# Result tiles of an expert mixture: two stores of 64 queries each in place of one store over both row numbers

## The chip, the cores and the metric

The kernel runs on one core of a Trainium2 chip. The metric is the time of one execution on the device in microseconds, the median of several runs. The engines are named as the profile names them: PE (TensorE, matrix multiplication; PEld is its weight load), DVE (VectorE), ACT (ScalarE), POOL (GpSimd) and SP (SyncE, which here only issues DMAs). A core has 16 DMA engines, which carry out what SP issues.

## The reference

Three stages follow each other. Linear attention over 4 batches, 8 heads, 576 positions and 64 channels; then a gated two-layer block on the 2304 tokens; then a mixture of four experts, each weighted by the token's normalised domain probability.

```
attn:  kv = k_s^T v  per batch and head;   out = q_s kv
x = attn_out.transpose(0, 2, 1, 3).reshape(2304, 512)
moe:   h = (x @ w1) * (x @ w2) @ w3;   x = h @ w_out
moe2:  p = domain_probs / sum;   for each expert e of 4:
         out += p[:, e] * (relu(x @ e1[e]) @ e2[e])
```

The result has 2304 rows of 512 float32.

## The kernel before

**Passes.** The change lies in the last stage, the experts, from about 484 us on. The 2304 tokens are worked in three groups (`pr` = 0, 1, 2) of 768 tokens, and each group takes 8 passes (`NGE` = 8: four experts, the hidden width in two parts). So there are 24 passes `n`. A pass has `layer1(n)` (lines 727 to 786, matmuls at line 765) and `layer2(n)` (lines 788 to 814, matmuls at lines 112 to 114). `layer2` goes over the group's six result tiles in the order 3, 4, 5, 0, 1, 2; for each it adds the pass's part into the tile `acc[T]` (128 partitions of 512 float32, 256 KB) on DVE, at line 802 in a group's first pass and at line 806 in the others. In a group's last pass (n = 7, 15, 23) the tile is complete and `store(T)` is called at line 811.

**Weights.** `load_e(n)` (lines 555 to 565) brings a pass's weights by four DMAs of 512 KB on SP's queue: two of `e1r` (line 561), two of `e2r` (line 564). Both share three buffers (pool `raw`), so a load waits until an older one has been split. `e1_steps(n)` (line 694) splits `e1r` into high and low parts `eg`, on ACT at line 107 and on DVE at line 108; the matmuls of `layer1` read these. At a group's change `tset` (line 567) brings the next group's tokens, `yp` (line 571).

**Order.** A scheduler of the framework fixes each engine's order when the program is built, and an engine works through its own list in that order. SP does likewise: a DMA that is issued late holds up those behind it in SP's list, the weight loads among them. In the list the stores of a group stand together, ahead of the loads of `e1r` and `e2r` for the pass after next; the third group's stores end the program.

**Rows of the result.** A row number `n` of 0 to 8 and a query number `q` of 0 to 63 give one of a batch's 576 rows, row 9q + n. A tile holds two row numbers, 2t and 2t + 1, with 64 queries each: partitions 0 to 63 and 64 to 127. In DRAM the 64 rows of one row number lie 9 rows (18 KB) apart. `store(t)` therefore writes a view in which the row number is the first dimension: 2 x 64 x 512, from a tile of 128 x 512. Where the two row numbers belong to two batches (tiles 4 and 13 of 18), it writes two halves of 64 x 512 instead.

Of the kernel before, what the change touches and what calls it, by code (L numbers as in the profile page):

```python
# [61 lines left out]
def linear_attention_moe_kernel(ctx: ExitStack, tc, q, k, v, w1, w2, w3, wo, dp, e1, e2, out):  # L62
    nc = tc.nc
    w1, w2, w3, wo = (w.bitcast(I32) for w in (w1, w2, w3, wo))
    B, H, S, D = q.shape
# [9 lines left out]
    QP, QR = 64, 9  # L75
# [290 lines left out]
    def rows_cols(unit):  # L366
        c, kt = unit
        return ((kt,), 0) if c == "A" else ((kt, kt + 1), 4 if c == "B" else 6)
# [3 lines left out]
    for unit in UNITS:  # L372
        kts, _ = rows_cols(unit)
# [4 lines left out]
    n = 0  # L378
# [224 lines left out]
    for u, unit in enumerate(UNITS):  # L603
# [9 lines left out]
        for x, kt in enumerate(kts):  # L613
            for y in range(ni):
                i = i0 + y
# [65 lines left out]
    acc = {}  # L681

    def store(t):
        rows = [(2 * t + hf) for hf in range(2)]
        (b0, n0), (b1, _) = (divmod(i, QR) for i in rows)
        if b0 == b1:
            dst = out[S * b0:S * b0 + S].rearrange("(q n) d -> n q d", n=QR)
            nc.sync.dma_start(out=dst[n0:n0 + 2], in_=acc[t])
        else:
            for hf, i in enumerate(rows):  # L690
                dst = out[S * (i // QR):S * (i // QR) + S].rearrange("(q n) d -> n q d", n=QR)
                nc.sync.dma_start(out=dst[i % QR], in_=acc[t][QP * hf:QP * hf + QP])

    def e1_steps(n):

# [92 lines left out]
    def layer2(n, h, steps):  # L788
        w, pr, e = ew[n], n // NGE, n % NGE // 2
        order = [3, 4, 5, 0, 1, 2]  # L790
        for x, tt in enumerate(order):
            th, o = tt // 3, P * (tt % 3)
            T = 6 * pr + tt
            ps = bank(ps_h, "op")
            for i, (hf, u) in enumerate(((0, 0), (0, 1), (1, 0), (1, 1))):
                g, wg = h[u, hf, th], w["e2", hf, u]
                mm3(
                    ps, g[:, 0, o:o + P], g[:, 1, o:o + P], wg[:, 0], wg[:, 1], i == 0, i == 3
                )
            if n % NGE == 0:  # L800
                acc[T] = acp.tile([P, DM], F32, tag="acc", name="acc")
                nc.vector.tensor_scalar(
                    out=acc[T], in0=ps, scalar1=prob[:, T, e:e + 1], scalar2=None, op0=ALU.mult
                )
            else:
                nc.vector.scalar_tensor_tensor(  # L806
                    out=acc[T], in0=ps, scalar=prob[:, T, e:e + 1], in1=acc[T],
                    op0=ALU.mult, op1=ALU.add,
                )
            if n % NGE == NGE - 1:  # L810
                store(T)
            for f in steps[len(steps) * x // 6:len(steps) * (x + 1) // 6]:
                for g in f:
                    g()
# [44 lines left out]
```

## Time and profile before

| what | value |
|---|---|
| time, median of 3 runs | 1251.23 us (1251.16 to 1251.36) |
| the profiled execution | 1249.22 us |
| its span, first to last instruction | 1247.4 us |
| mean granted TensorE clock | 0.98 |
| PE busy | 1168.6 us, 94% of the span |
| DVE, ACT, POOL busy | 748.0, 497.6, 56.2 us |
| stores of results (256 KB; 128 KB) | 16; 4 |

The span is divided by stages: attention and the folding of the weights at first, the gated block to about 484 us, the experts after that. Times in the rows below are counted from the start of the span. "Idle before" an instruction is time in which its engine did nothing else, with the instruction or DMA that ended the wait behind the arrow. For SP the number behind a DMA's start is how long its issue held SP, not how long the transfer took. The DMA share of a window is the mean busy share of the 16 DMA engines.

### The profile page before, as it was taken

The page shows a single profiled execution, that of the slowest core. Times are in us where ns is not written, and L with a number is a line of the kernel's source. Part 1 is how long each engine was busy: PE and PEld are TensorE (multiplying, and loading weights), DVE is VectorE, ACT ScalarE, POOL GpSimd, SP SyncE. Part 2 cuts the span into 40 slices and gives each one's busy share as a digit, 9 for nine tenths or more (in the row PEclk, how much of TensorE's full clock was granted, in tenths as well). Part 3 has the DMA queues.
Part 4 walks back from the last instruction along what each step waited for, and adds up shares of the span by engine and source line. Part 5 has one row for each costly group of instructions (what it writes and reads, how often), then busy time and mean ns, then how long its engine had stood idle before and what let it go on. Part 6 is the DMA issues. An engine that isn't in the chain of part 4 may idle for free.

```text
span 1247.4 us, 15277 instructions
## 1 busy us (share of the span) xinstructions
PE 1168.6 (94%) x5728; PEld 1015.7 (81%) x5728; DVE 748.0 (60%) x1332; ACT 497.6 (40%) x1084; POOL 56.2 (5%) x76
## 2 busy tenths in 40 slices
PE   4789989999999999999999979999999799999994
PEld 3567868788878988999999979999999689999983
DVE  7988953423152147666667856666678376666641
ACT  4676544323241244333335433333344243333320
POOL 0020322201100000000000000000000000000000
PEclk9899999999999999999999989999999999999997
DMA  9949656527346431212121422211222312212001
GB/s 315 335 109 267 218 183 190 150 94 256 112 136 228 152 127 68 69 68 68 68 68 68 142 95 68 68 68 68 68 68 72 110 49 68 70 69 67 21 1 50
DMA packets 98394, 142.63 MB, mean 114 GB/s; under 512 B 26384, under 2 KB 63760, under 8 KB 98320
## 3 DMA queue, kind: packets, MB, share of 16 engines
q1 hardware_dynamic: 98320, 141.65, 34.6%
q8 instruction: 45, 0.74, 0.2%
q14 instruction: 29, 0.24, 0.1%
HBM read 123.81 MB, written 17.83 MB: 114 GB/s over the span
## 4 chain that ended last, share of the span: by engine, by line
PE 85%; DMA 7%; ACT 3%; DVE 2%; SPq 1%; issue 1%; POOL 0%; ACTq 0%; DVEq 0%; POOLq 0%
PE hp L765 26%; PE op L114 11%; PE op L112 11%; PE op L113 11%; PE ab L112 5%; PE ab L114 5%; PE ab L113 5%; PE y L112 2%; PE y L114 2%; PE y L113 2%; DMA e1r<-in_moe_w_dram 2%; PE kv L241 1%; DMA kr<-in_k_dram 1%; DMA f<-in_moe_w_dram 1%; ACT qe L270 1%; PE xp L318 1%
## 5 line engine op out<-in xcount | busy, mean ns | idle before, releaser
L765 PE MATMUL hp<-t,eg 128*128 128x384 f32 x2016 | 369.5, 335 | 3.3 <-DVE eg L108 2.1
L765 PEld LDWEIGHTS hp<-t,eg 128*128 128x128 f32 x2016 | 352.5, 188 | 14.7 <-DVE eg L108 2.7
L112 PE MATMUL op<-e2g,h 128*128 128x512 f32 x576 | 227.4, 395 | 15.0 <-ACT h L744 15.0
L113 PE MATMUL op<-e2g,h 128*128 128x512 f32 x576 | 227.7, 395 | 0.0
L114 PE MATMUL op<-e2g,h 128*128 128x512 f32 x576 | 223.8, 396 | 0.0
L740 ACT ACTIVATE p<-hp 128x384 f32<-128x384 f32 x144 | 65.2, 491 | 301.6 <-PE hp L765 301.6
L806 DVE SCALAR_TENSOR_TENSOR acc<-op,prob,acc 128x512 f32<-128x512 f32 x126 | 94.4, 749 | 128.8 <-PE op L114 125.2
L108 DVE TENSOR_TENSOR eg<-e1r,eg 128x512 fp32r<-128x512 f32 x168 | 114.7, 689 | 82.5 <-ACT eg L107 82.5
L107 ACT ACTIVATE eg<-e1r 128x512 fp32r<-128x512 f32 x168 | 104.9, 630 | 110.9 <-PE hp L765 47.5
L112 PEld LDWEIGHTS op<-e2g,h 128*128 128x128 f32 x576 | 109.3, 190 | 36.1 <-ACT h L744 15.7
L114 PEld LDWEIGHTS op<-e2g,h 128*128 128x128 f32 x576 | 109.2, 190 | 23.0
L113 PEld LDWEIGHTS op<-e2g,h 128*128 128x128 f32 x576 | 109.2, 190 | 21.0
L112 PE MATMUL ab<-x,wg 128*128 128x512 f32 (+1 forms) x320 | 120.9, 379 | 2.3 <-ACT ah L485 1.2
L113 PE MATMUL ab<-x,wg 128*128 128x512 f32 (+1 forms) x320 | 119.5, 373 | 0.0
L114 PE MATMUL ab<-x,wg 128*128 128x512 f32 (+1 forms) x320 | 119.1, 372 | 0.0
L753 DVE TENSOR_TENSOR p<-hp,p 128x384 f32<-128x384 f32 x144 | 79.6, 554 | 17.4 <-ACT p L740 17.2
L486 DVE TENSOR_TENSOR ah<-ab,ah 128x512 f32<-128x512 f32 (+1 forms) x40 | 25.3, 634 | 96.3 <-PE ab L114 87.2
L745 DVE SCALAR_TENSOR_TENSOR h<-p,h 128x384 fp32r<-128x384 f32 x144 | 76.3, 553 | 0.4
L744 ACT ACTIVATE h<-p 128x384 fp32r<-128x384 f32 x144 | 71.8, 514 | 7.8 <-DVE p L753 6.7
L112 PEld LDWEIGHTS ab<-x,wg 128*128 128x128 f32 x320 | 60.5, 189 | 14.8 <-ACT ah L485 2.4
L114 PEld LDWEIGHTS ab<-x,wg 128*128 128x128 f32 x320 | 60.6, 189 | 10.9 <-DVE wg L108 0.5
L113 PEld LDWEIGHTS ab<-x,wg 128*128 128x128 f32 x320 | 60.7, 190 | 10.0 <-DVE x L108 0.4
(86 smaller groups left out, 1273.6 us busy)
## 6 DMA issues: line engine op xcount, KB each, us to landing
wg<-w SPq DMA_DIRECT2D x64, 512.0 KB
e1r<-in_moe_w_dram SPq DMA_DIRECT2D x48, 512.0 KB
e2r<-in_moe_w_dram SPq DMA_DIRECT2D x48, 512.0 KB
f<-in_moe_w_dram SPq DMA_DIRECT2D x32, 512.0 KB
w<-wg SPq DMA_DIRECT2D x16, 512.0 KB
qr<-in_q_dram SPq DMA_DIRECT2D x16, 288.0 KB
yp<-yd SPq DMA_DIRECT2D x3, 1536.0 KB
f<-in_moe_w_out_dram SPq DMA_DIRECT2D x8, 512.0 KB
```

What stands on the lines that cost most here:

```text
L107: i = nc.scalar.activation(out=hi, in_=src, func=ACTF.Copy)
L108: eng.tensor_tensor(out=lo, in0=src, in1=hi.bitcast(F32), op=ALU.subtract)
L112: nc.tensor.matmul(out=ps, lhsT=w_hi, rhs=r_hi, start=first, stop=False)
L113: nc.tensor.matmul(out=ps, lhsT=w_hi, rhs=r_lo, start=False, stop=False)
L114: nc.tensor.matmul(out=ps, lhsT=w_lo, rhs=r_hi, start=False, stop=last)
L486: nc.vector.tensor_tensor(out=ah[:, 1, 0:n], in0=pss[1][:, 0:n], in1=ah[:, 0, 0:n], op=ALU.mult)
L740: nc.scalar.activation(out=p, in_=src, func=ACTF.Copy)
L744: nc.scalar.activation(out=g[:, 0], in_=src, func=ACTF.Relu)
L745: nc.vector.scalar_tensor_tensor(out=g[:, 1], in0=src, scalar=0.0, in1=g[:, 0].bitcast(F32), op0=ALU.max, op1=ALU.subtract,)
L753: nc.vector.tensor_tensor(out=p, in0=src, in1=p, op=ALU.add)
L765: nc.tensor.matmul(out=o, lhsT=wl[2 * sw + kt], rhs=t[b][:, kt, st], start=new and kt == 0 and i == 0, stop=kt == 1 and i == 2, skip_group ...
L806: nc.vector.scalar_tensor_tensor(out=acc[T], in0=ps, scalar=prob[:, T, e:e + 1], in1=acc[T], op0=ALU.mult, op1=ALU.add,)
```

## The change

`store` no longer asks whether both row numbers lie in one batch. It issues two DMAs for every tile, one for each row number, each from 64 partitions of the tile to 64 rows of the result.

```
     def store(t):
-        rows = [(2 * t + hf) for hf in range(2)]
-        (b0, n0), (b1, _) = (divmod(i, QR) for i in rows)
-        if b0 == b1:
-            dst = out[S * b0:S * b0 + S].rearrange("(q n) d -> n q d", n=QR)
-            nc.sync.dma_start(out=dst[n0:n0 + 2], in_=acc[t])
-        else:
-            for hf, i in enumerate(rows):
-                dst = out[S * (i // QR):S * (i // QR) + S].rearrange("(q n) d -> n q d", n=QR)
-                nc.sync.dma_start(out=dst[i % QR], in_=acc[t][QP * hf:QP * hf + QP])
+        for hf in range(2):
+            b, n = divmod(2 * t + hf, QR)
+            dst = out[S * b:S * b + S].rearrange("(q n) d -> n q d", n=QR)
+            nc.sync.dma_start(out=dst[n], in_=acc[t][QP * hf:QP * hf + QP])
```

The lists of PE, DVE, ACT and POOL are the same before and after. On SP, at the end of the first token group, these rows stood before (`out_dram<-acc` is a store, `yp<-yd` the next group's tokens):

```order
L561 DMA e1r<-in_moe_w_dram 128x4x256 x2
L571 DMA yp<-yd 128x4x768
L564 DMA e2r<-in_moe_w_dram 128x2x512 x2
L688 DMA out_dram<-acc 2x64x512
L692 DMA out_dram<-acc 64x512 x2
L688 DMA out_dram<-acc 2x64x512 x4
L561 DMA e1r<-in_moe_w_dram 128x4x256 x2
L564 DMA e2r<-in_moe_w_dram 128x2x512 x2
```

On SP at the same place now:

```order
L561 DMA e1r<-in_moe_w_dram 128x4x256 x2
L571 DMA yp<-yd 128x4x768
L564 DMA e2r<-in_moe_w_dram 128x2x512 x2
L687 DMA out_dram<-acc 64x512 x12
L561 DMA e1r<-in_moe_w_dram 128x4x256 x2
L564 DMA e2r<-in_moe_w_dram 128x2x512 x2
```

Seven stores have become twelve of one shape, at the same place in the list. At the end of the program SP's list read:

```order
L561 DMA e1r<-in_moe_w_dram 128x4x256 x2
L564 DMA e2r<-in_moe_w_dram 128x2x512 x2
L688 DMA out_dram<-acc 2x64x512 x4
L692 DMA out_dram<-acc 64x512 x2
L688 DMA out_dram<-acc 2x64x512
L854 UNCONDITIONAL_BRANCH
```

And on SP at the end of the program now:

```order
L564 DMA e2r<-in_moe_w_dram 128x2x512 x2
L561 DMA e1r<-in_moe_w_dram 128x4x256 x2
L564 DMA e2r<-in_moe_w_dram 128x2x512 x2
L687 DMA out_dram<-acc 64x512 x12
L849 UNCONDITIONAL_BRANCH
```

Here too twelve half stores stand where five whole ones and two halves stood. At the end of the second group, which has no tile across a batch, six whole stores have become twelve halves.

## Rows read from the trace of the kernel before

**Rows 1.** Page, part 1: busy time (share of the span) and instructions.

```profile
PE 1168.6 (94%) x5728; PEld 1015.7 (81%) x5728; DVE 748.0 (60%) x1332; ACT 497.6 (40%) x1084; POOL 56.2 (5%) x76
```

**Rows 2.** Waits of PE, 484 to 1248 us: total us, times, longest.

```profile
PE op L112 <- ACT h L744: 15.0, 2, 8.6
```

**Rows 3.** Timeline, PE: start, us, engine, line, operation, tiles, count [idle before].

```profile
737.05 0.79 PE L112 MATMUL op<-e2g,h 128*128 128x512 f32 x1 [6.34 <-ACT h L744]
...
997.74 0.80 PE L112 MATMUL op<-e2g,h 128*128 128x512 f32 x1 [8.63 <-ACT h L744]
```

**Rows 4.** Timeline, ACT: splits of e1r in both pauses and in another pass.

```profile
735.96 0.63 ACT L107 ACTIVATE eg<-e1r 128x512 fp32r<-128x512 f32 x1 [10.20 <-DMA e1r<-in_moe_w_dram]
...
996.65 0.63 ACT L107 ACTIVATE eg<-e1r 128x512 fp32r<-128x512 f32 x1 [13.18 <-DMA e1r<-in_moe_w_dram]
...
765.78 0.63 ACT L107 ACTIVATE eg<-e1r 128x512 fp32r<-128x512 f32 x1 [0.39 <-PE hp L765]
```

**Rows 5.** Timeline, SP: DMA issues, 691 to 1022 us.

```profile
691.01 0.92 SPq L561 DMA_DIRECT2D e1r<-in_moe_w_dram  x2
...
705.18 1.91 SPq L692 DMA_DIRECT2D out_dram<-acc  x2
711.04 10.80 SPq L688 DMA_DIRECT2D out_dram<-acc  x4
721.94 6.70 SPq L561 DMA_DIRECT2D e1r<-in_moe_w_dram  x2
...
761.76 0.92 SPq L561 DMA_DIRECT2D e1r<-in_moe_w_dram  x2
...
792.92 1.02 SPq L561 DMA_DIRECT2D e1r<-in_moe_w_dram  x2
...
949.35 0.92 SPq L561 DMA_DIRECT2D e1r<-in_moe_w_dram  x2
...
961.53 19.82 SPq L688 DMA_DIRECT2D out_dram<-acc  x6
981.44 8.01 SPq L561 DMA_DIRECT2D e1r<-in_moe_w_dram  x2
...
1021.90 0.92 SPq L561 DMA_DIRECT2D e1r<-in_moe_w_dram  x2
```

**Rows 6.** Windows: us, busy time of five engines, PEclk, DMA share, GB/s.

```profile
716.00:721.00 5.00, 5.00 (x24) 4.21 (x23) 2.80 (x5) 2.35 (x4) 0.00 (x0) 1.00 0.13 51
...
1233.00:1234.50 1.50, 0.00 (x0) 0.00 (x0) 0.00 (x0) 0.00 (x0) 0.00 (x0) 0.87 0.82 178
1234.50:1236.00 1.50, 0.00 (x0) 0.00 (x0) 0.00 (x0) 0.00 (x0) 0.00 (x0) 0.50 0.34 76
...
1246.00:1247.40 1.40, 0.00 (x0) 0.00 (x0) 0.00 (x0) 0.00 (x0) 0.00 (x0) 0.50 0.02 6
```

**Rows 7.** Windows over the two stretches at half clock (columns as above).

```profile
735.75:742.58 6.83, 5.53 (x13) 4.37 (x14) 4.68 (x9) 2.83 (x6) 0.00 (x0) 0.50 0.08 28
991.75:1001.99 10.24, 4.25 (x10) 3.42 (x11) 4.61 (x8) 2.84 (x6) 0.00 (x0) 0.50 0.39 136
```

**Rows 8.** Tail: SP and DVE in the timeline, and one window.

```profile
1217.47 9.88 SPq L688 DMA_DIRECT2D out_dram<-acc  x4
...
1233.09 0.55 SPq L688 DMA_DIRECT2D out_dram<-acc  x1
...
1226.44 0.75 DVE L806 SCALAR_TENSOR_TENSOR acc<-op,prob,acc 128x512 f32<-128x512 f32 x1 [1.97 <-PE op L114]
1229.16 0.75 DVE L806 SCALAR_TENSOR_TENSOR acc<-op,prob,acc 128x512 f32<-128x512 f32 x1 [1.97 <-PE op L114]
...
1218.00:1219.00 1.00, 1.00 (x7) 0.81 (x6) 0.72 (x1) 0.00 (x0) 0.00 (x0) 1.00 0.05 12
```

**Rows 9.** Instructions on tile acc: duration ns min/median/max, first and last start.

```profile
L688 SPq DMA_DIRECT2D out_dram<-acc x16: 512/540/2848, 703.2 to 1233.1; - x16
L692 SPq DMA_DIRECT2D out_dram<-acc x4: 542/954/4917, 705.2 to 1232.4; - x4
```

## Prediction

> **What bounds the kernel now.** I read the page first: TensorE is busy for 1168.6 us, 94% of the span [rows 1]. So TensorE is the bound nearly everywhere, and a change to stores can pay only where TensorE stands still. The stores come in the expert part, from 484 us on. There the table of waits has one line for TensorE: 15.0 us in two waits [rows 2]. The timeline gives their places: 6.34 us of idleness end at 737.05 and 8.63 us end at 997.74 [rows 3]. Both matmuls wait for ScalarE, and ScalarE in its turn had stood for 10.20 and 13.18 us on the DMA that brings e1r, the expert weights of the next pass [rows 4]. After 1229.9, when the last addition into acc ends, no engine works, and the span runs on for 17.5 us, to 1247.4 [rows 6, 8]. So there are three places: two pauses in the middle and the tail.
>
> All three lie behind stores. The timeline of SP's queue shows six result tiles stored at 703 to 722, six at 961 to 981, six at 1217 to 1234 [rows 5, 8, 9]. In the windows a whole-tile store keeps 0.13 of the DMA engines busy and moves 51 GB/s [rows 6]: 0.13 of 16 is two engines. A tile of 256 KB (262,144 bytes) then takes 262,144 / 51,000 = 5.14 us. A group holds five or six of these, 26 or 31 us on the same two engines, and the loads of e1r behind them need all engines. Their issue takes 6.70 and 8.01 us instead of 0.92, so the queue itself is held up [rows 5].
>
> **What a half tile does** is shown too, since tiles 4 and 13 of 18 cross a batch and are stored in two halves already (L692). When the two halves of tile 13 get their turn in the tail, the windows show 0.82 of the engines busy and 178 GB/s, then 0.34 and 76 GB/s, then the two-engine picture again [rows 6]. Half tiles therefore use all engines, and the pair takes about 3.0 us (1233 to 1236), beside a backlog on two engines.
>
> **The change, part by part.**
>
> *Order.* Compute on TensorE, VectorE, ScalarE and GpSimd keeps its order; only SP differs, with twelve half stores per group where six or seven transfers stood. Sixteen issues more.
>
> *Issues added.* A whole store's issue takes 540 ns at the median, a half's 954 ns over four, among them 4917 ns for one that stood behind four whole stores [rows 8, 9]; the least are 512 and 542 ns [rows 9]. The undisturbed pair cost 1.91 us [rows 5]. Taking 0.55 to 0.95 us for each, 16 more make 9 to 15 us on SP's queue. That lies beside work: in a group the six tiles come over 18 us as VectorE finishes them, and SP waits between. What stands behind the waiting SP are the e1r and e2r loads. Only the second half of the last tile delays them, 0.55 to 0.95 us: the first e1r load moves from 721.94 to about 722.7.
>
> *First pause.* Elsewhere a load of e1r issued at 761.76 is used at 765.78, 4.02 us later, and ScalarE's wait there is for TensorE and not for the DMA [rows 4, 5]. So the load issued at 722.7 is there at 726.7, or at 729.7 if it stands behind the whole 3.0 us of the last pair. ScalarE starts to wait at 735.96 - 10.20 = 725.76. Its 10.20 us cost TensorE 6.34, so 3.86 us of its waiting are free: TensorE notices nothing until 729.6. The pause goes entirely, at the worst all but 0.1 us.
>
> *Second pause.* The same with 13.18 - 8.63 = 4.55 us free. ScalarE starts to wait at 983.47; the load would be issued near 981 and arrive at 985 to 988, against a limit of 988.0.
>
> *What the pauses cost in all.* After them TensorE's granted clock is 0.50, that is 1.2 of 2.4 GHz, and TensorE works 5.53 and 4.25 us at it [rows 7]. The whole price shows in the distance between e1r loads. One pass takes 792.92 - 761.76 = 31.16 us. The two passes from 691.01 to 761.76 take 70.75, that is 8.43 over 62.32; the two from 949.35 to 1021.90 take 72.55, that is 10.23 over [rows 5]. Together **18.7 us**. Bounds: idleness plus half of the slow stretch, 14.97 + 0.5 x 9.78 = 19.9; idleness alone less 1 us for each load that comes late, 13.0. I take 18.7, since it is a distance measured over the whole disturbance. With no idleness I expect no drop of the clock either: both slow stretches begin in or just before the end of a pause [rows 3, 7].
>
> *Tail.* Now: the last whole store is issued at 1233.09, queued behind the others, and the last bytes go at about 1246.2 (6 GB/s over the last 1.4 us are 8.4 KB, 0.16 us at 51 GB/s) [rows 6, 8]. After the change the pair of the last tile is issued at 1229.94 and 1230.5, when the acc is ready; hardly anything is queued any more, since a pair is gone in 3.0 us and tiles come 1229.16 - 1226.44 = 2.72 us apart [rows 8]. First bytes come 1.3 us after an issue: 1217.47, and 12 KB moved by 1219, at 51 GB/s a quarter of a microsecond [rows 8]. Bounds for the bytes: 1.5 us for 256 KB at the 178 GB/s of the window, so the end at 1229.94 + 1.3 + 1.5 = 1232.7; or 3.0 us counted from the second half's first bytes, 1230.5 + 1.3 + 3.0 = 1234.8. I take 1234.2, near the slow end, because that row is the pair itself. What follows the last byte (1.2 us) stays. Gain 1246.2 - 1234.2 = **12.0 us**, bounds 11.4 and 13.5.
>
> *Sum.* 18.7 + 12.0 = 30.7 us off the profiled execution of 1249.22, which is its span of 1247.4 and 1.8 around it: 1218.5. The median is 1251.23, 2.0 above that execution, so **1220.5 us**. Own range: gains of 13.0 + 11.4 = 24.4 to 19.9 + 13.5 = 33.4 us, so 1217.8 to 1226.8.
>
> **A rule that speaks against it.** Rows 6 show one tile on two engines and its halves on nearly all. The Trainium skill (DMA: Bandwidth & Descriptors, Rules for kernel authors) says of two transfers to disjoint partition halves not to bother, because both spread over all 16 engines anyway and serialize, and to use one transfer over 128 partitions. By that rule the sum would be zero and the time that of rival B; its reason, a whole transfer on 16 engines, is not what this trace shows.
>
> **The rivals.**
>
> *A: the pauses stay, only the tail gains.* The table of waits could mislead, and e1r could be late for its buffer or for HBM traffic. For it: in every pass the load is issued only 4 us before its use. Against it: in both pauses the load had been issued 14.0 and 15.2 us before its use, and the two engines were full. Price: 12.0 us alone, 1239.2 us.
>
> *B: no gain, because a pair is no faster than a tile.* The mechanism: the rate is set by something that all stores share, the writing of 2 KB rows 18 KB apart in HBM, and not by the number of engines. Then halves go at 51 GB/s together, the bytes and the backlog stay, and one more issue of 0.6 us stands at the end: 1251.8 us. Against it: 178 GB/s in rows 6 with the same rows and the same stride.
>
> *C: slower, because a half store blocks SP.* If 4.92 us is what a 16-engine store's issue costs [rows 9], and not the backlog before it, twelve take 59 us from the first store at 703.2 [rows 9] and e1r is issued at 762 instead of 722. It arrives at 766, 30 us after 735.96, twice; the tail ends about 30 us later as well: some 1340 us. It decides from the mean issue: above (731.9 - 703.2) / 12 = 2.4 us the load comes later than now (731.9 is 735.96 less the 4.02). Against it: the pair at 705.18 took 1.91 us for both.
>
> *D: slower, because the rate goes with the size*, a half of 128 KB taking the 5.14 us of a whole. Twelve halves occupy the engines for 62 us per group instead of 26 to 31, and each of the three places is 31 to 36 us later: some 1350 us. Rows 6 speak against it as against B.
>
> **How the numbers follow.** Forecast 0.84, A 0.06, B 0.04, C 0.04, D 0.02. Faster by over 0.2% (2.5 us, about what a measurement can tell from no change): forecast and A, 0.90. Within: B, 0.04. Slower: C and D, 0.06. The range needs 0.8; the forecast's own bounds hold nearly all of its 0.84, so I give 1217.5 to 1227.0.
>
> **What would show it.** In the new profile: no wait of TensorE over 1 us after 484 us, and no stretch at 0.50 between 484 us and the end of compute; e1r loads 31 to 32 us apart throughout, also near 722 and 950; issues of e1r under 1.5 us; the DMA share in the store groups in short bursts over 0.5 and never 0.13 for microseconds on end; span end less than 6 us after the last addition into acc. If the pauses remain with an idle SP queue, A is right; if the share stays at 0.13, B; if issues of half stores take over 2.4 us each, C. The forecast is wrong in size if the load in the second pause comes after its limit of 988 by the new timeline's count, or if the last pair needs much more than 4.3 us from its first issue.

## The result, and the profile of the changed kernel

The changed kernel takes 1219.11 us (median of 4 runs, 1217.84 to 1220.65), the kernel before 1251.20 us (median of 4 too). The ratio is 0.9745 with a 95% interval of 0.9728 to 0.9762. The profiled execution took 1217.84 us, with a span of 1216.1 us.

The page of the changed kernel, parts 1 and 2 (busy time; then the clock granted to TensorE in 40 equal slices of the span, in tenths of full speed):

```profile
PE 1166.0 (96%) x5728; PEld 1014.4 (83%) x5728; DVE 750.4 (62%) x1332; ACT 497.7 (41%) x1084; POOL 52.4 (4%) x76
...
PEclk9889998999999999999999999999999999999999
```

Against [rows 1], TensorE's busy time is nearly the same; the span has lost what stood beside it. After 484 us the table of TensorE's waits, which had one line with 15.0 us in [rows 2], is empty. The windows of us, busy times of five engines, clock, DMA share and GB/s, first round the first change of token group, then round the second:

```profile
690.00:762.00 72.00, 72.00 (x367) 65.57 (x367) 55.13 (x94) 34.91 (x67) 0.00 (x0) 1.00 0.39 121
...
950.00:1022.00 72.00, 72.00 (x360) 64.64 (x359) 49.91 (x85) 27.61 (x56) 0.00 (x0) 1.00 0.31 95
```

The same windows of the kernel before:

```profile
690.00:762.00 72.00, 65.66 (x317) 58.57 (x316) 46.48 (x78) 27.51 (x54) 0.00 (x0) 0.95 0.30 103
...
950.00:1022.00 72.00, 63.37 (x307) 56.43 (x306) 42.07 (x72) 25.03 (x52) 0.00 (x0) 0.93 0.23 81
```

TensorE is now busy in all of the 72 us, at a granted clock of 1.00, which is 2.4 GHz; before it stood still for 6.3 and 8.6 us and the mean clock was 0.95 and 0.93. The queue of SP in the changed kernel (start, how long the issues held SP, line, tiles, count), which answers to [rows 5]:

```profile
661.62 0.92 SPq L561 DMA_DIRECT2D e1r<-in_moe_w_dram  x2
...
693.44 0.92 SPq L561 DMA_DIRECT2D e1r<-in_moe_w_dram  x2
...
705.62 19.25 SPq L687 DMA_DIRECT2D out_dram<-acc  x12
724.97 1.13 SPq L561 DMA_DIRECT2D e1r<-in_moe_w_dram  x2
...
755.02 0.92 SPq L561 DMA_DIRECT2D e1r<-in_moe_w_dram  x2
...
942.61 0.92 SPq L561 DMA_DIRECT2D e1r<-in_moe_w_dram  x2
...
954.79 18.21 SPq L687 DMA_DIRECT2D out_dram<-acc  x12
973.09 1.33 SPq L561 DMA_DIRECT2D e1r<-in_moe_w_dram  x2
...
1004.24 0.92 SPq L561 DMA_DIRECT2D e1r<-in_moe_w_dram  x2
```

Read the loads of e1r behind the stores: their two issues hold SP for 1.13 and 1.33 us, where it had been 6.70 and 8.01 us. The two passes from 693.44 to 755.02 take 61.58 us (70.75 before), those from 942.61 to 1004.24 take 61.63 us (72.55 before): 9.17 and 10.92 us, together 20.1 us.

The instructions on the tile acc (duration in ns, min/median/max; under them us from issue to landing), which answer to [rows 9], and the windows and the last addition of the tail, which answer to [rows 6, 8]:

```profile
L687 SPq DMA_DIRECT2D out_dram<-acc x36: 466/569/766, 705.6 to 1212.8; - x36
...
DMA to landing us min/median/max: 2.2/2.4/3.5
```

```profile
715.00:717.00 2.00, 2.00 (x14) 2.00 (x13) 0.00 (x0) 1.33 (x4) 0.00 (x0) 1.00 0.86 199
717.00:721.00 4.00, 4.00 (x20) 3.33 (x19) 1.44 (x2) 0.99 (x4) 0.00 (x0) 1.00 0.04 9
...
1213.00:1215.00 2.00, 0.00 (x0) 0.00 (x0) 0.00 (x0) 0.00 (x0) 0.00 (x0) 1.00 0.56 131
1215.00:1216.10 1.10, 0.00 (x0) 0.00 (x0) 0.00 (x0) 0.00 (x0) 0.00 (x0) 0.61 0.00 0
...
1211.51 0.75 DVE L801 SCALAR_TENSOR_TENSOR acc<-op,prob,acc 128x512 f32<-128x512 f32 x1 [1.97 <-PE op L114]
```

Stores are now short bursts (0.86 of the engines, 199 GB/s, then almost nothing) where 0.13 and 51 GB/s had gone on for tens of microseconds. The last addition ends at 1212.26 and the span at 1216.1: the tail is 3.8 us, before it was 17.5.

### The profile page after: what moved, and what is told of

It reads as the page before. It is cut to its first block, busy times and chain, and to the rows that moved or that the text cites. A ratio compares the mean times of both kernels' runs of the same rounds, so it can differ in the third digit from the quotient of the medians.

```text
span 1216.1 us, 15296 instructions
## 1 busy us (share of the span) xinstructions
PE 1166.0 (96%) x5728; PEld 1014.4 (83%) x5728; DVE 750.4 (62%) x1332; ACT 497.7 (41%) x1084; POOL 52.4 (4%) x76
## 4 chain that ended last, share of the span: by engine, by line
PE 88%; DMA 4%; ACT 4%; DVE 2%; SPq 1%; issue 1%; ACTq 0%; DVEq 0%
PE hp L760 28%; PE op L114 11%; PE op L113 11%; PE op L112 11%; PE ab L112 5%; PE ab L114 5%; PE ab L113 5%; PE y L112 3%; PE y L114 2%; PE y L113 2%; DMA kr<-in_k_dram 2%; PE kv L241 1%; DMA f<-in_moe_w_dram 1%; PE xp L318 1%; ACT qe L270 1%; DMA f<-in_moe_w_out_dram 1%
## 5 line engine op out<-in xcount | busy, mean ns | idle before, releaser
L114 PEld LDWEIGHTS op<-e2g,h 128*128 128x128 f32 x576 | 108.1, 188 | 22.5
L113 PEld LDWEIGHTS op<-e2g,h 128*128 128x128 f32 x576 | 108.1, 188 | 20.7
L112 PEld LDWEIGHTS op<-e2g,h 128*128 128x128 f32 x576 | 108.1, 188 | 20.0
```

The source lines that it names most:

```text
L112: nc.tensor.matmul(out=ps, lhsT=w_hi, rhs=r_hi, start=first, stop=False)
L113: nc.tensor.matmul(out=ps, lhsT=w_hi, rhs=r_lo, start=False, stop=False)
L114: nc.tensor.matmul(out=ps, lhsT=w_lo, rhs=r_hi, start=False, stop=last)
```

## The experiments

All kernels ran against the kernel before, on one chip per group of runs; its medians there were 1251.2 to 1251.7 us. The diffs stand against the changed kernel. In three kernels (e1, e2, e3) the rows of the result stand in other places, as their expectations say; bytes and compute are the same.

**Two halves, but a first dimension of 2 (e1).** The theory: how many DMA engines a store gets follows from the first dimension of its view. The rival: it is the smaller size, or the split itself, that pays.

```
-            dst = out[S * b:S * b + S].rearrange("(q n) d -> n q d", n=QR)
+            dst = out[S * b:S * b + S].rearrange("(q a n) d -> n a q d", n=QR, a=2)
```

> Two stores per tile as in the changed kernel, the same bytes from the same partitions, but each view has a first dimension of 2 (2 x 32 x 512): the queries of a half are written in another order, so rows of the result stand in other places. Theory (the engines that a store uses follow from the first dimension of its view): DMA share 0.13, 51 GB/s, backlog as before, pauses of TensorE near 737 and 997 back: 1250 to 1253 us. Rival (it is the split into two smaller transfers that pays): 1218 to 1221 us, no pause.

Measured: 1262.01 us, ratio 1.0089 (1.0068 to 1.0110). The window in the first store group and the one in the tail, then its SP queue and its stores:

```profile
716.00:722.00 6.00, 6.00 (x30) 5.17 (x29) 1.77 (x3) 2.72 (x6) 0.00 (x0) 1.00 0.13 51
1240.00:1258.00 18.00, 0.00 (x0) 0.00 (x0) 0.00 (x0) 0.00 (x0) 0.00 (x0) 0.50 0.13 51
...
729.72 3.92 SPq L561 DMA_DIRECT2D e1r<-in_moe_w_dram  x2
...
L687 SPq DMA_DIRECT2D out_dram<-acc x36: 507/1101/4320, 705.7 to 1246.5; - x36
```

Two engines again, with transfers of the same size and number as in the changed kernel; the waits of TensorE are back, 20.4 us in two. The rival falls. That the kernel is 10 us slower than before, and not level, I had not reckoned with. One part is that tiles 4 and 13 go over two engines here as well, which before the change were the only halves on all of them. Groups one and three so have six slow tiles in place of five, by estimate 5.14 us more each. The tail fits that: it is 23.2 us long (17.5 before). The pauses fit it only in part: by the distances between e1r loads the first costs 3.6 us more than before the change, and the second 1.7 us more, although all six tiles of its group were slow before too. That rest was not explained.

**First dimension of 4 (e2).** The same edit with `a=4`.

> As the run with first dimension 2, but 4 x 16 x 512 (rows of the result again in another order). Theory: four engines, share 0.25, 102 GB/s, a tile in 2.6 us, which is no longer than the 2.7 us between tiles: no backlog, no pause of TensorE, the tail longer than that of the changed kernel by 1 to 1.5 us: 1219 to 1222 us. Rival (only all engines will do): share below 0.5 and a pause of 2 us or more left at both places: 1225 to 1240 us.

Measured: 1224.61 us, ratio 0.9791 (0.9774 to 0.9809). Two windows of its tail:

```profile
1209.00:1217.00 8.00, 5.68 (x26) 4.37 (x24) 2.25 (x3) 0.00 (x0) 0.00 (x0) 1.00 0.26 84
1217.00:1223.00 6.00, 0.00 (x0) 0.00 (x0) 0.00 (x0) 0.00 (x0) 0.00 (x0) 0.61 0.26 89
```

A quarter of the 16 engines is busy, as the theory says. TensorE waits 0.4 us in all, so four engines are nearly enough for the pauses. But they move 84 to 89 GB/s and not 102 (in the first 4 us, from 1205 to 1209, only 57 to 66, at the same share), a tile takes 262,144 / 86,000 = 3.0 us against 2.72 between tiles, and a backlog grows: the tail is 9.9 us, 6.1 longer than the changed kernel's. Direction right, size of the tail missed by 5 us. Why four engines move less than twice what two do was not settled.

**One store per tile, first dimension of 64 (e3).**

```
-        for hf in range(2):
+        (b0, n0), (b1, _) = divmod(2 * t, QR), divmod(2 * t + 1, QR)
+        if b0 == b1:
+            dst = out[S * b0:S * b0 + S].rearrange("(q n) d -> q n d", n=QR)
+            nc.sync.dma_start(out=dst[:, n0:n0 + 2], in_=acc[t])
+            return
+        for hf in range(2):
```

> One store per tile of 256 KB as before (two only where a tile crosses a batch), but with the 64 queries as first dimension of the view and the two row numbers inside it; the source gives its 128 partitions in order, so rows of the result stand in other places. Theory (first dimension): all engines, no pause, tail as short as with two stores: 1218 to 1221 us. Rival (a transfer of 256 KB is slow, halves are fast): 1250 to 1252 us.

Measured: 1217.53 us, ratio 0.9732 (0.9717 to 0.9746). Its stores, and a window with the last one:

```profile
L687 SPq DMA_DIRECT2D out_dram<-acc x16: 538/542/597, 705.0 to 1211.7; - x16
...
1213.00:1214.00 1.00, 0.00 (x0) 0.00 (x0) 0.00 (x0) 0.00 (x0) 0.00 (x0) 1.00 0.62 242
```

Sixteen transfers of 256 KB, as many and as large as before the change, move at 242 GB/s and none holds SP for over 0.6 us. TensorE waits for nothing, the tail is 3.3 us. So neither size nor number decides here; with e1, that leaves the first dimension of the view. This view also puts neighbouring rows of the result side by side and moves its bytes with fewer engines busy than the halves do (242 GB/s at a share of 0.62, against 199 at 0.86); which of its differences does that was not tested. To use this with the rows in their right places, the queries would have to lie in partition 2q + n of the tile, which the earlier stages would have to provide; that was not tried.

**The last group alone (e4), the first two alone (e5).** Ahead of the two half stores of the changed kernel:

```
+        (b0, n0), (b1, _) = divmod(2 * t, QR), divmod(2 * t + 1, QR)
+        if t < 12 and b0 == b1:      # e5: t >= 12
+            dst = out[S * b0:S * b0 + S].rearrange("(q n) d -> n q d", n=QR)
+            nc.sync.dma_start(out=dst[n0:n0 + 2], in_=acc[t])
+            return
```

> Half stores in the last token group alone, whole stores in the first two. Theory: the pauses stay, the tail goes from 17.5 to 3.8 us: 1251.2 - 13.7 = 1237.5 us. Rival (the long tail is an echo of a backlog that begins in the earlier groups): more than 1245 us.

> Half stores in the first two token groups, whole stores in the last. Theory: the pauses go, 20.1 us by the distances between e1r loads, the tail stays at 17.5 us: 1251.2 - 20.1 = 1231.1 us, and with the run that splits the last group alone the two gains add up to that of the change. Rival (the pauses come from the traffic of the token change and not from stores): a pause remains and the time is above 1240 us.

Measured: 1237.60 us, ratio 0.9891 (0.9874 to 0.9907), and 1231.40 us, ratio 0.9839 (0.9823 to 0.9856). The waits of TensorE after 484 us in e4, and the e1r load behind its first whole stores; then the last addition of e5, whose span is 1230.7 us:

```profile
PE op L112 <- ACT h L744: 15.0, 2, 8.7
...
724.23 6.69 SPq L561 DMA_DIRECT2D e1r<-in_moe_w_dram  x2
...
1212.24 0.75 DVE L806 SCALAR_TENSOR_TENSOR acc<-op,prob,acc 128x512 f32<-128x512 f32 x1 [1.97 <-PE op L114]
```

e4 keeps both pauses and has a tail of 4.0 us; e5 has no wait of TensorE and a tail of 17.7 us. The gains, 14.1 and 19.8 us, add up to 33.9, about the change's own (32.1 in the first comparison, 34.4 in e8). So the tail and the two pauses are independent of each other, and both rivals fall. The two pauses were not taken apart.

**Four stores per tile (e6).**

```
-        for hf in range(2):
-            b, n = divmod(2 * t + hf, QR)
+        for hf in range(4):
+            b, n = divmod(2 * t + hf // 2, QR)
+            o = 32 * (hf % 2)
...
-            nc.sync.dma_start(out=dst[n], in_=acc[t][QP * hf:QP * hf + QP])
+            nc.sync.dma_start(out=dst[n, o:o + 32], in_=acc[t][32 * hf:32 * hf + 32])
```

> Four stores per tile of 32 queries each, 64 KB, 72 in all. Theory: each issue costs SP 0.5 to 0.6 us and nothing else; the last tile's four issues put the e1r load back by 1.1 us, inside ScalarE's slack of 2.8 us and more; tail 0.5 to 1 us longer: 1219 to 1221 us. Rival (the issue of a store that uses all engines is what costs): issues of 1 us and more, pauses of TensorE back: above 1225 us.

Measured: 1218.22 us, ratio 0.9742 (0.9727 to 0.9756). Its stores:

```profile
L688 SPq DMA_DIRECT2D out_dram<-acc x72: 314/422/1530, 705.3 to 1213.2; - x72
```

Twice the issues of the changed kernel cost little; one takes 0.42 us, less than expected. The tail is 4.5 us, 0.7 longer. Against e8, the changed kernel on the same chip, the median is 1.5 us higher: in the profiles 0.7 of it is the tail, and another 0.75 is there already before the first store (the e1r load at 661.29 us, in e8 at 660.54). Rival C of the prediction, an issue that is dear by itself, falls with this and with e1: the same 36 issues took 569 ns at the median with a free way and 1101 ns behind a backlog.

**Whole stores on GpSimd's queue (e7).** The block of e4 for all tiles, with `nc.gpsimd` for `nc.sync`.

> Whole stores as before, but issued on the queue of GpSimd, which has nothing else to do there. Rival of the theory (SP's blocked queue is what delays e1r, the two engines are not): e1r is issued on time, the pauses vanish, the tail stays: 1231 us. Theory (the two engines are full, whoever issues): e1r is issued on time but lands late, pauses of some us remain, the tail stays: 1235 to 1251 us. If the queue of GpSimd spreads a store in another way, the DMA share shows it, and then pauses and tail go as in the changed kernel: 1219 to 1222 us.

Measured: 1231.74 us, ratio 0.9844 (0.9829 to 0.9859). The SP queue at the first change of group, the waits of ScalarE and TensorE, the landing of the stores, a window between loads and one at the end, when the last store is alone:

```profile
722.24 1.02 SPq L561 DMA_DIRECT2D e1r<-in_moe_w_dram  x2
...
ACT eg L107 <- DMA e1r<-in_moe_w_dram: 13.7, 3, 7.2
...
PE op L112 <- ACT h L744: 4.4, 2, 2.7
...
DMA to landing us min/median/max: 7.3/10.2/12.5
...
713.00:721.00 8.00, 8.00 (x40) 7.01 (x39) 2.96 (x5) 4.24 (x9) 1.55 (x2) 1.00 0.25 48
...
1224.00:1226.00 2.00, 0.00 (x0) 0.00 (x0) 0.00 (x0) 0.00 (x0) 0.00 (x0) 0.50 0.11 45
```

The time is that of the rival, but not its mechanism: pauses are left, and the tail is 11.7 us, not 17.5. The stores go another way here. Up to about 719 us two of them are in flight (issued at 711.62 and 712.95, landed 9.1 and 12.5 us later) and keep 0.25 of the engines busy at 48 GB/s; the last store, alone from 1223 us on, keeps 0.11 busy at 45 GB/s. So one store takes about two engines on this queue too, but two stores run side by side, on four. A store lands after 10.2 us at the median. So the case is not a clean one for either side. Part of it holds: e1r is issued on time and held up by nothing on SP, and still ScalarE waits up to 7.2 us for it, so a blocked queue is not needed to make the load late. Engines that are busy with stores are the likely reason, but no run shows this by itself. How much of the old pauses was the blocked queue of SP and how much the two full engines stays open.

**The changed kernel again (e8).** No edit.

> The changed kernel once more. In its first profile the first e1r load of the experts comes 2.4 us later than before, in a part that the change does not touch, and its four times spread over 2.8 us. Theory (that part varies from run to run): another position of the same load in this profile, by 1 us or more, and the time follows it; 1217 to 1221 us. Rival (the change moves it): the same 2.4 us again, in this profile and in those of the other kernels with half stores.

Measured: 1216.76 us, ratio 0.9726 (0.9712 to 0.9741). The third load of e1r, issued near the end of the gated block, in the kernel before, in the changed one, in e8, in e4 and in e2, one fence each:

```profile
469.82 0.92 SPq L561 DMA_DIRECT2D e1r<-in_moe_w_dram  x2
```

```profile
472.33 0.92 SPq L561 DMA_DIRECT2D e1r<-in_moe_w_dram  x2
```

```profile
471.17 0.92 SPq L561 DMA_DIRECT2D e1r<-in_moe_w_dram  x2
```

```profile
472.22 0.92 SPq L561 DMA_DIRECT2D e1r<-in_moe_w_dram  x2
```

```profile
474.93 0.92 SPq L561 DMA_DIRECT2D e1r<-in_moe_w_dram  x2
```

This load comes ahead of all stores, and no kernel here changes what precedes it. It stands between 469.8 and 474.9 us in the profiles, with whole stores in the first groups (469.82, 472.22) and with halves (471.17, 472.33, 474.93), and 1.2 us apart for one and the same kernel, whose profiled time follows (1216.79 against 1217.84 us). So the 2.5 us that had looked like a loss of the change lie within what the profiles differ by, 5.1 us. What that hangs on was not looked into. The median of 1216.76 lies 0.2 us under the range expected here.

**The last two halves on two queues (e9).**

```
-            nc.sync.dma_start(out=dst[n], in_=acc[t][QP * hf:QP * hf + QP])
+            eng = nc.scalar if t == 14 and hf else nc.sync
+            eng.dma_start(out=dst[n], in_=acc[t][QP * hf:QP * hf + QP])
```

> The changed kernel, but the second half of the very last tile (14) is issued on ScalarE's queue, which is idle by then, so that both halves are issued at once. Theory: the second half is issued 0.5 us earlier, the tail goes from 3.8 to 3.3 us, the time by the same 0.5 us, which the spread of the runs hides: 1216 to 1221 us. Rival (the two halves limit each other on the DMA engines): the tail stays at 3.8 us.

Measured: 1217.49 us, ratio 0.9730 (0.9714 to 0.9746), which cannot be told from the changed kernel. The issue and the window of the last bytes; then half a microsecond of the last bytes in the changed kernel, where the halves go one after the other:

```profile
1211.89 0.56 ACTq L688 DMA_DIRECT2D out_dram<-acc  x1
...
1213.00:1214.00 1.00, 0.00 (x0) 0.00 (x0) 0.00 (x0) 0.00 (x0) 0.00 (x0) 1.00 0.94 250
```

```profile
1213.50:1214.00 0.50, 0.00 (x0) 0.00 (x0) 0.00 (x0) 0.00 (x0) 0.00 (x0) 1.00 0.94 209
```

The half is issued 0.5 us earlier, but the tail is 3.6 us, 0.2 shorter: one half at a time, or nearly so, had kept 0.94 of the engines busy already (209 GB/s), and both at once do not keep more busy (250 GB/s). Theory and rival each hold in part.

## Why the prediction was right

Forecast 1220.5 us, range 1217.5 to 1227.0; measured 1219.1. The mechanism was right; both terms of the sum were too small, and part of the close hit is luck. Point by point:

- **The bound and the three places.** Right. The tail and the pair of pauses each paid for itself (e4, e5), and nothing else in the experts changed: the passes between the group changes take the same 187.6 us in all profiles.
- **Two engines for a whole tile, all for a half.** Right, and now by dose: first dimensions of 2, 4 and 64 gave shares of 0.13, 0.26 and 0.6 to 0.9 (e1, e2, e3 and the change). The prediction had this from four half stores alone and left open whether the size or the view decides. It is the view. The Trainium skill (DMA: Bandwidth & Descriptors, Why a DMA increments its semaphore by 16 and not by 1) gives the rule: a transfer gets the largest number of engines up to 16 that divides the size of the slowest dimension on both sides. For 2 and 128 that is 2, for 4 and 64 it is 4, for 64 and 128 it is 16; the traces agree. The Trainium skill's rule against halves (same page, Rules for kernel authors), which the prediction weighed, gives as its reason that both spread over all engines. It does not fit the kernel before, whose single transfer had two of 16; it fits e3, where the single transfer has all of them and 1217.5 us are level with the 1216.8 to 1219.1 us of the halves.
- **Issues added.** Right: 0.55 to 0.95 us foreseen, 0.57 measured. Counted as in the kernel before (2.4 us less) the first e1r load was issued at 722.5, with 722.7 foreseen.
- **The pauses go.** Right. At the first change ScalarE does not wait for e1r at all (1.0 us in the profile of e8); at the second it waits 1.76 us, within its slack of 4.55 us, and TensorE does not notice. Counted as in the kernel before, that load is used at 985.2, with 985 to 988 foreseen. ScalarE in the changed kernel:

```profile
728.88 0.63 ACT L107 ACTIVATE eg<-e1r 128x512 fp32r<-128x512 f32 x1 [0.69 <-PE hp L760]
...
978.48 0.63 ACT L107 ACTIVATE eg<-e1r 128x512 fp32r<-128x512 f32 x1 [1.76 <-DMA e1r<-in_moe_w_dram]
```

- **The price of the pauses.** Mis-sized: 18.7 us foreseen, 20.1 measured, over the bound of 19.9. The step that failed is the yardstick of two ordinary passes, 62.32 us. At a change of group the loads are spaced otherwise: the pass that brings the new tokens is 0.66 us longer (661.62 to 693.44 is 31.82 us), and the two after it are 0.7 us shorter together (61.58). I compared the disturbed pair with passes from the middle of a group.
- **The tail.** Mis-sized: 12.0 foreseen, 17.5 - 3.8 = 13.7 measured, 0.2 over the bound. I counted 4.3 us from the first issue of the last pair to its last byte, by a pair that ran beside a backlog on two engines; alone it took at most 2.7 (issued at 1212.29; no byte moves after 1215.0). The bound with the early end, 1232.7, which is 2.8 us after the issue, was the better estimate.
- **The sum.** 20.1 + 13.7 = 33.8 us, above the prediction's own bound of 33.4. Less 2.4 us by which the untouched part came later in that execution: 31.4, which is 1249.22 less 1217.84. The two terms that were too small and this chance delay nearly cancelled, so the forecast of 1220.5 is closer than its terms were. In e8 the same kernel took 1216.76 us, 0.7 under the range: that the measured time lies inside is owed in part to this luck.
- **The rivals.** A falls with e5 and with the empty table of waits; B and D with the 199 GB/s of the changed kernel; C with the issues of 0.57 us there and of 0.42 us in e6.

## What to carry to other kernels

Look at the DMA share of a window in which only one kind of transfer runs: 0.13 for tens of microseconds is two engines of 16, and then the shape of the view is the first thing to look at, not the size. Put a dimension first in both views that gives all engines, as 64 did here (of lengths above 4 only 32, in e6, and 64 were run for the result), or split the transfer along the short one. In this kernel a slow store cost nothing where it ran; it cost where a load stood behind it, and at the end of the program, where nothing hid it.

## What the runs showed that I had not expected

- A backlog on two engines comes back into the issuing queue: in the kernel before, most issues of stores take about 0.5 us, and three of them, each behind a group's earlier stores, 2.7, 2.8 and 4.9 us. In e1, with nothing but such stores, the median issue was 1.10 us, against 0.57 us in the changed kernel.
- Four engines move 84 to 89 GB/s where two move 51 (e2); the cause is open.
- On GpSimd's queue two stores of the same view run side by side: share 0.25 at 48 GB/s in e7, and 0.11 at 45 GB/s for one alone. On SP's queue a backlog of them stayed at 0.13 and 51 GB/s.
- Even with a free way one load of e1r comes late: ScalarE waits 1.76 us for it at the second change of group in the changed kernel, which costs TensorE nothing; another such wait, of 1.8 us at 635.9 us, has no store near it.
